# Attention scores and values as 64-row products on each half of TensorE's rows

## The chip, the cores and the metric

The kernel runs on one core of a Trainium2 chip. The time is the device time of one execution in microseconds (us), 590.46 us as the median of three runs before the change. The profile is of one further execution, taken by the hardware profiler. Its engines are called PE (TensorE's matmuls), PEld (TensorE's weight loads, which overlap matmuls), DVE (VectorE), ACT (ScalarE), POOL (GpSimd) and SP (SyncE, which here issues DMAs).

## The reference, cut to what matters

Attention with keys and values averaged over 8 neighbouring positions is followed by a mixture of 8 experts, of which each token takes one. The second part isn't touched.

```python
B, H, S, D = (8, 8, 576, 64); Sp = 72
k_p = k.reshape(B, H, Sp, 8, D).mean(axis=3)
v_p = v.reshape(B, H, Sp, 8, D).mean(axis=3)
scores = q @ k_p.T / sqrt(D)                 # 576 x 72 for each of 64 heads
attn = softmax(scores)
x = (attn @ v_p)  ->  (B * S, H * D) = (4608, 512)
e = argmax(x @ w_gate + modality_bias[modality_id])
out = softmax value of e  *  relu(x @ w1[e]) @ w2[e]
```

All of it is in float32. A matmul of float32 operands that is not a transpose shows in the trace as two records of weight load and matmul; a transpose shows as one of each.

## The kernel before, in words

The first 172 us are the attention, the rest is the experts, which begin as the last attention steps end. Attention handles 36 tiles of 128 tokens. Two tiles make a step (`steps`, 16 of them); besides, there are four mixed steps of one tile, which holds the last 64 tokens of one batch and the last 64 of the next. Each step does its eight heads in two parts `w` of four heads.

For a step and a part, `q_pe` transposes q. It takes two tokens' 64 dimensions at once, so that in `qt` rows 0 to 63 hold one token's dimensions and rows 64 to 127 the other's: `qt` has two 128-token tiles stacked on the 128 rows that the matmul sums over. The keys `kt` are therefore kept twice, once with zeros in rows 64 to 127 and once with zeros in rows 0 to 63 (`kt[:, 0]` and `kt[:, 1]`, 576 columns each). `s_pe` (L586 to L604) multiplies, for each of four heads, `qt` (128 rows, 128 columns as weights) with both copies side by side: 128 rows, 2 x 72 = 144 columns. Half of the operand is zeros.

`s_dve` takes row maxima and subtracts them, `s_act` takes the exponentials and sorts them: per tile and pair of heads 128 of the 144 columns go to one 128-column block of `pe` (main), the other 16 to a tail. `t_pe` and `t_act` transpose the four blocks of a tile to `pt`, `t4_pe` and `t4_act` transpose the tails of the step and copy rows 0 to 63 to `pt4z[0]` and rows 64 to 127 to `pt4z[1]`; the other rows of these stay zero.

`a_pe` (L653 to L671) multiplies per pair of heads a block of `pt` with `vw`, whose columns are 2 x 73: for each head of the pair 64 value columns, 8 columns of the router's product and one column of ones, with zeros in the rows of the other head (`m_a` and `m_b` are the masks; row 72 is where the second head begins). Two products of `pt4z` with `v4` add the tails. That is 4 + 2 products of 128 rows and 146 columns for a tile. In mixed steps each product is done twice, for 64 tokens each, on one half of TensorE's columns.

`load_v`, `pool_v` and `v_operand` bring the values into this layout; `v_gate` makes the router's columns (L459, and L460 for the tails, which has 64 rows).

Nothing reorders the work: each engine does its instructions in the order in which the program's loop over steps (L980 to L1062) writes them. In that order the products stand between transposes: `t_pe`, `s_pe` of the second part, `t4_pe`, `a_pe`, `q_pe`, `s_pe` of the next step's first part. SP issues all loads in the order of a table, in one queue, and waits there for the tile that a load overwrites to be free.

## Time and profile before

| what | us |
|---|---|
| median of 3 runs (lowest, highest) | 590.46 (590.09, 590.72) |
| the profiled execution | 590.98 |
| its span, first to last instruction | 589.3 |
| PE, PEld busy | 570.9, 499.6 |
| DVE, ACT, POOL busy | 372.7, 273.8, 187.2 |

The span is 1.7 us shorter than the execution's time. The granted TensorE clock is 0.998 over the span. Matmuls overlap: one of 144 columns is shown with 289 ns though the next starts 0.12 us later, so a PE that reads as busy can still have lost time between two products. Rows of groups give busy time in us, the mean duration of one in ns, and the engine's idle time before them. `128*128 128x144` means weights on 128 rows and 128 columns, and a moving operand of 128 rows and 144 columns; `64*128` are weights on 64 rows.

### The profile page before, as it was taken

How to read it: one execution, taken by the hardware profiler on the slowest of the kernel's cores; microseconds unless marked ns; L12 is line 12 of the kernel's file. 1: busy time of each engine (PE TensorE's matmuls, PEld its weight loads, DVE VectorE, ACT ScalarE, POOL GpSimd, SP SyncE). 2: the span in 40 equal slices, each digit the busy share in tenths (PEclk: the TensorE clock that was granted, in tenths of full speed). 3: DMA queues.
4: the chain of work that ended last, by engine and by line, in shares of the span. 5: the costliest groups of instructions: out<-in, count | busy, mean ns of one | idle time of the engine just before them, and what ended most of it. 6: DMA issues, size and time to landing. Idle time of an engine off the chain costs nothing.

```text
span 589.3 us, 12333 instructions
## 1 busy us (share of the span) xinstructions
PE 570.9 (97%) x3539; PEld 499.6 (85%) x3539; DVE 372.7 (63%) x945; ACT 273.8 (46%) x652; POOL 187.2 (32%) x290
## 2 busy tenths in 40 slices
PE   6999999999999999999999999999999999999995
PEld 5789789988898888888888888888888888888894
DVE  5877898788966766557455446855455487555311
ACT  2767677788552333333333336633333474334210
POOL 7679967765000323112112102112102113212101
PEclk9999999999999999999999999999999999999999
DMA  8999979995311744232232277242234843241101
GB/s 257 306 323 282 360 219 309 304 313 171 103 54 39 263 169 121 79 125 91 82 118 95 86 230 241 91 125 91 87 111 137 255 158 105 91 146 54 38 3 55
DMA packets 83426, 92.60 MB, mean 157 GB/s; under 512 B 17871, under 2 KB 58319, under 8 KB 83344
## 3 DMA queue, kind: packets, MB, share of 16 engines
q1 hardware_dynamic: 77424, 72.24, 39.2%
q0 software_dynamic: 5920, 19.44, 9.9%
q8 instruction: 30, 0.49, 0.4%
q14 instruction: 52, 0.43, 0.2%
HBM read 123.06 MB, written 27.58 MB: 256 GB/s over the span
## 4 chain that ended last, share of the span: by engine, by line
PE 82%; DVE 7%; DMA 5%; ACT 2%; issue 1%; SPq 1%; POOLq 0%; POOL 0%; DVEq 0%; ACTq 0%
PE op L1345 33%; PE hp L209 20%; PE hp L214 10%; PE av L667 4%; PE hp L183 3%; PE sc L603 3%; DMA q<-in_q_dram 3%; PE av L671 2%; DMA v<-in_v_dram 2%; PE pp L632 2%; PE pq L578 2%; PE ph L183 1%; DVE mx L610 1%; DVE hl L141 1%; DMA out_dram<-obw,slw 1%
## 5 line engine op out<-in xcount | busy, mean ns | idle before, releaser
L209 PE MATMUL hp<-xhl,hl 128*128 128x512 f32 x512 | 126.6, 390 | 0.0
L1321 POOL DMA_INDIRECT out_dram<-ob,sidx x34 | 36.8, 1083 | 263.6 <-DVE ob L1315 191.2
L209 PEld LDWEIGHTS hp<-xhl,hl 128*128 128x128 f32 x512 | 96.1, 188 | 19.9
L217 ACT COPY ht<-hp 128x256 f32<-128x256 f32 x128 | 47.3, 373 | 138.7 <-PE hp L214 112.3
L218 DVE TENSOR_TENSOR ht<-ht,hp 128x256 f32<-128x256 f32 x128 | 52.8, 420 | 92.5 <-ACT ht L217 89.4
L1345 PE MATMUL op<-hl,hx 128*128 128x512 f32 x429 | 104.8, 392 | 0.0
L1345 PEld LDWEIGHTS op<-hl,hx 128*128 128x128 f32 x429 | 78.5, 189 | 14.6
L1345 PE MATMUL op<-hl,hh 128*128 128x512 f32 x256 | 79.8, 393 | 0.0
L214 PEld LDWEIGHTS hp<-xhl,hl 128*128 128x128 f32 x512 | 69.8, 191 | 4.9
L214 PE MATMUL hp<-xhl,hl 128*128 128x256 f32 x512 | 71.5, 283 | 0.0
L1345 PEld LDWEIGHTS op<-hl,hh 128*128 128x128 f32 x256 | 46.0, 189 | 7.8
L667 PE MATMUL av<-vw,pt 128*128 128x146 f32 (+1 forms) x320 | 49.2, 293 | 1.4 <-DVE xb L700 1.3
L1345 PE MATMUL op<-hl,hlo 128*128 128x512 f32 x128 | 49.9, 390 | 0.0
L144 POOL DMA_INDIRECT xg<-xs,gidx x36 | 38.6, 1073 | 29.0 <-DMA raw<-in_moe_w_dram 13.8
L667 PEld LDWEIGHTS av<-vw,pt 128*128 128x128 f32 (+1 forms) x320 | 39.6, 180 | 3.4 <-DVE xb L700 1.0
L223 DVE SCALAR_TENSOR_TENSOR hx<-ht,hx 128x256 fp32r<-128x256 f32 x64 | 27.2, 427 | 18.8 <-DVEq L1350 15.7
L223 DVE SCALAR_TENSOR_TENSOR hlo<-ht,hh 128x256 fp32r<-128x256 f32 x64 | 27.1, 425 | 18.5 <-DVEq L1350 15.3
L603 PE MATMUL sc<-kt,qt 128*128 128x144 f32 x256 | 37.4, 289 | 0.6 <-DVE rs L798 0.3
L603 PEld LDWEIGHTS sc<-kt,qt 128*128 128x128 f32 x256 | 33.2, 190 | 1.6 <-DVE rs L798 0.5
L610 DVE TENSOR_REDUCE mx<-sc 128x8 f32<-128x576 f32 (+1 forms) x40 | 27.7, 692 | 7.5 <-PE sc L603 6.9
L671 PE MATMUL av<-vw,pt 128*128 128x146 f32 (+1 forms) x160 | 30.0, 290 | 0.0
L221 ACT ACTIVATE hx<-ht 128x256 fp32r<-128x256 f32 x64 | 26.2, 419 | 7.4 <-DVE ht L218 5.7
(279 smaller groups left out, 907.7 us busy)
## 6 DMA issues: line engine op xcount, KB each, us to landing
raw<-in_moe_w_dram SPq DMA_DIRECT2D x288, 256.0 KB
xs<-xb SPq DMA_DIRECT2D x16, 528.0 KB
scr<-xg SPq DMA_DIRECT2D x29, 256.0 KB
k<-in_k_dram SPq DMA_DIRECT2D x7, 1024.0 KB
v<-in_v_dram SPq DMA_DIRECT2D x7, 1024.0 KB
q<-in_q_dram SPq DMA_DIRECT2D x7, 1024.0 KB
y<-scr SPq DMA_DIRECT2D x108, 64.0 KB
v<-in_v_dram SPq DMA_DIRECT2D x16, 128.0 KB
```

The costliest lines, as they stand in the source:

```text
L144: nc.gpsimd.indirect_dma_start(out=x, out_offset=None, in_=xs[0:rows, :], in_offset=IndirectOffsetOnAxis(idx[:, col:col + 1].bitcast(U32), 0),
L209: nc.tensor.matmul(hp[g % 2], hl[g][:, 0, d * P:(d + 1) * P], ab[:, d, :, 0:SLOT], start=(d == 0), stop=False)
L214: nc.tensor.matmul(hp[g % 2][:, 0:SLOT], hl[g][:, 1, d * P:(d + 1) * P], ab[:, d, 0, 0:SLOT], start=False, stop=(d == ND - 1))
L217: nc.scalar.copy(hts[g % 2], hp[g % 2][:, SLOT:2 * SLOT])
L218: nc.vector.tensor_add(hts[g % 2], hts[g % 2], hp[g % 2][:, 0:SLOT])
L223: nc.vector.scalar_tensor_tensor(hlo, hts[g % 2], 0.0, hh.bitcast(F32), op0=ALU.max, op1=ALU.subtract)
L603: nc.tensor.matmul(dst, qt[:, i, :], kt[b % NB][:, :, h * SPL:(h + 1) * SPL], start=True, stop=True)
L610: nc.vector.reduce_max(mx, scv, axis=AX.X)
L667: nc.tensor.matmul(av[hs, u, 2 * VC * gg:2 * VC * (gg + 1)], pt[:, c, hs], vw[y][:, c].rearrange("p a x -> p (a x)"), start=(gg == 0), sto ...
L671: nc.tensor.matmul(dst4[hs], pt4[:, hs], v4[y][:, 2 * u:2 * u + 2, :], start=False, stop=True)
L1321: nc.gpsimd.indirect_dma_start(out=out[:, :], out_offset=IndirectOffsetOnAxis(idx.bitcast(U32), 0), in_=ob, in_offset=None, bounds_check=N ...
L1345: nc.tensor.matmul(ot, l[:, ts_], hl[f][:, w, D:2 * D], start=(f == 0 and n == 0), stop=(f == NF - 1 and n == 2))
```

## The change

`kt` and `vw` lose their zero halves. `kt` holds the same keys in rows 0 to 63 and in rows 64 to 127. `s_pe` makes two products where there was one: rows 0 to 63 of `qt` with rows 0 to 63 of `kt`, and rows 64 to 127 with rows 64 to 127, of 72 columns each, into different banks of PSUM (index `a`). For the values a pair is now head `c` and head `4 + c`: the first 64 of a head's 72 pooled positions lie on one half of the rows, and the last 8 in the tail. `a_pe` makes 8 products of 64 rows and 73 columns, and for the tails two of 64 rows and 4 x 73 = 292 columns. In mixed steps products have 64 rows and 64 weight columns, so that four of them cover the array. The two halves stand next to each other in the program.

With that, loads of `v` are cut in two (64 rows each) and those of the tails in four; `v_operand` has one copy instead of two scaled ones; the transposed tails are written with a mask (`m_z`) to both `pt4z` in full height; memsets of `kt` and `pt4z` go away.

PE around `s_pe` of a step's second part (one step of two tiles; `pp` are transposes of the exponentials, `sc` the scores and, at L644 or L645, the transposed tails, `pv` transposes of pooled values, `av` the values' products), before:

```order
L632 MATMUL pp_771<-ident,pe_676 128x128 x4
L603 MATMUL sc_1_781<-kt_133,qt_1_709 128x2x72 x4
L644 MATMUL sc_0_729<-ident,pe_676 128x128
L443 MATMUL pv_792<-ident,vp_658 128x128 x2
L444 MATMUL pv_792<-ident,vp_2_659 64x128
L667 MATMUL av_800<-vw_137,pt_776 128x146 x2
L671 MATMUL av_800<-vw_139,pt_0_134 128x2x73
L667 MATMUL av_800<-vw_137,pt_776 128x146 x2
L671 MATMUL av_800<-vw_139,pt_0_134 128x2x73
```

and of the change:

```order
L634 MATMUL pp_844<-ident,pe_730 128x128 x4
L602 MATMUL sc_1_854<-kt_137,qt_1_775 128x72 x8
L645 MATMUL sc_0_795<-ident,pe_730 128x128
L443 MATMUL pv_868<-ident,vp_712 128x128 x2
L444 MATMUL pv_868<-ident,vp_2_713 64x128
L668 MATMUL av_876<-vw_141,pt_849 128x73 x8
L673 MATMUL av_876<-vw_143,pt_0_138 128x292 x2
```

The order of the groups is the same. Four products of scores became eight, six of values became ten, and the transposes of 128 rows before, between and behind them stayed where they were.

ACT at the same place (`pt_0` and `pt_1` are the two `pt4z`), before:

```order
L651 COPY pt_0_134<-sc_0_729 64x128
L651 COPY pt_1_135<-sc_0_729 64x128
L436 ACTIVATE vw_136<-vp_658,m_a 128x4x64
L437 ACTIVATE vw_136<-vp_658,m_b 128x4x64
L447 COPY vt_796<-pv_792 128x256
```

and of the change:

```order
L652 ACTIVATE pt_0_138<-sc_0_795,m_z_144 128x128
L652 ACTIVATE pt_1_139<-sc_0_795,m_z_145 128x128
L437 COPY vw_140<-vp_712 128x4x64
L447 COPY vt_872<-pv_868 128x256
```

Two copies of 64 rows became scaled ones of 128 rows, and two scaled copies became one plain one.

The diff, cut to its core:

```diff
--- before.py
+++ after.py
@@ -265,17 +265,20 @@
-        def load_v(b, pairs=slice(0, NPAIR)):
+        def load_v(b, pairs=slice(0, 4)):
             if b not in vraw:
                 vraw[b] = big.tile([P, NPAIR, POOL * HD], F32, tag=f"s{V_SLOT[b % 3]}", name=f"v_{b}")
-            src = rows_of(v, b).rearrange("(c r) x -> r c x", r=2 * SPL)[0:P]
-            nc.sync.dma_start(vraw[b][:, pairs], src[:, pairs, :])
+            src = rows_of(v, b).rearrange("(h r) x -> r h x", r=SPL)[0:64]
+            for a in range(2):
+                nc.sync.dma_start(vraw[b][64 * a:64 * a + 64, pairs], src[:, 4 * a + pairs.start:4 * a + pairs.stop, :])
         def load_v4(b):
             t4 = ap.tile([P, POOL * HD], F32, tag="v4", bufs=2, name=f"v4_{b}")
-            src = rows_of(v, b).rearrange("(c r) x -> r c x", r=2 * SPL)[P:]
-            for z in range(2):
-                nc.sync.dma_start(t4[64 * z:64 * z + 64], src)
+            src = rows_of(v, b).rearrange("(h r) x -> r h x", r=SPL)[64:]
+            for a in range(2):
+                for z in range(2):
+                    r0 = 64 * a + 32 * z
+                    nc.sync.dma_start(t4[r0:r0 + 32], src[:, 4 * a:4 * a + 4, :])
             v4raw[b] = t4
         def load_q(b, parts=(0, 1)):
@@ -302,32 +305,30 @@
...
-        load_v(0, slice(2, NPAIR))
+        load_v(0, slice(2, 4))
...
-        kt = [ap.tile([P, 2, H * SPL], F32, name=f"kt{i}") for i in range(NB)]
+        kt = [ap.tile([P, H * SPL], F32, name=f"kt{i}") for i in range(NB)]
         pt4z = [ap.tile([P, P], F32, name=f"pt4_{z}") for z in range(2)]
-        vw = [ap.tile([P, NPAIR, 2, VC], F32, name=f"vw{i}") for i in range(NB)]
+        vw = [ap.tile([P, NPAIR, VC], F32, name=f"vw{i}") for i in range(NB)]
...
-        m_a = ap.tile([P, 1], F32, name="m_a")
-        m_b = ap.tile([P, 1], F32, name="m_b")
+        m_z = [ap.tile([P, 1], F32, name=f"m_z{z}") for z in range(2)]
...
-            nc.gpsimd.memset(pt4z[z][64 - 64 * z:128 - 64 * z], 0.0)
         for i in range(NB):
-            nc.gpsimd.memset(kt[i][0:64, 1, :], 0.0)
-            nc.gpsimd.memset(kt[i][64:128, 0, :], 0.0)
-            nc.gpsimd.tensor_copy(vw[i][:, :, 0, VC - 1], m_a.to_broadcast([P, NPAIR]))
-            nc.gpsimd.tensor_copy(vw[i][:, :, 1, VC - 1], m_b.to_broadcast([P, NPAIR]))
+            nc.gpsimd.memset(vw[i][:, :, VC - 1:VC], 1.0)
...
@@ -401,8 +402,8 @@
...
             x = slice(cs[0] * P, cs[0] * P + n)
-            nc.scalar.copy(dst[0:64, 0, x], pk[:, 0:n])
-            nc.scalar.copy(dst[64:128, 1, x], pk[:, 0:n])
+            nc.scalar.copy(dst[0:64, x], pk[:, 0:n])
+            nc.scalar.copy(dst[64:128, x], pk[:, 0:n])
         def pool_v(b):
             vp = ap.tile([P, NPAIR, HD], F32, tag="vp", bufs=2, name=f"vp_{b}")
@@ -433,8 +434,7 @@
         def v_operand(b):
...
             dw, d4 = vw[b % NB], v4[b % NB]
-            nc.scalar.activation(dw[:, :, 0, 0:HD], vp, AF.Copy, scale=m_a)
-            nc.scalar.activation(dw[:, :, 1, 0:HD], vp, AF.Copy, scale=m_b)
+            nc.scalar.copy(dw[:, :, 0:HD], vp)
...
@@ -457,10 +457,13 @@
...
-            nc.tensor.matmul(pg[:, 2, :], vt4, wg[0:64, 1::2, :], start=True, stop=True)
+            for a in range(2):
+                hs = slice(64 * a, 64 * a + 64)
+                nc.tensor.matmul(pg[hs, 2, :], vt4[:, hs], wg[0:64, 4 * a:4 * a + 4, :], start=True, stop=True)
             pgv = pg[:, 0:2, :].rearrange("p u (g a e) -> p (u g) a e", g=2, a=2)
-            nc.scalar.activation(dw[:, :, 0, HD:HD + E], pgv[:, :, 0, :], AF.Copy, scale=m_a)
-            nc.scalar.activation(dw[:, :, 1, HD:HD + E], pgv[:, :, 1, :], AF.Copy, scale=m_b)
+            for a in range(2):
+                hs = slice(64 * a, 64 * a + 64)
+                nc.scalar.copy(dw[hs, :, HD:HD + E], pgv[hs, :, a, :])
...
@@ -589,18 +592,15 @@
...
             if jj is None:
-                for u in range(2):
-                    c = 2 * w + u
-                    for z in range(2):
-                        hs = slice(64 * z, 64 * z + 64)
-                        src = kt[(b - 1 + z) % NB].rearrange("p a (h s) -> p (a h) s", s=SPL)[:, 2 * c:2 * c + H + 2:H + 1, :]
-                        nc.tensor.matmul(sc[hs, u, 0:2 * SPL].rearrange("p (a s) -> p a s", a=2), qt[:, u, hs], src,
-                                         start=True, stop=True)
+                tiles = [(u, slice(64 * z, 64 * z + 64), (b - 1 + z) % NB, 4 * w + 2 * u, 1) for u in range(2) for z in range(2)]
             else:
-                for i in range(4):
-                    dst = sc[:, i // 2, 0:4 * SPL].rearrange("p (t x) -> p t x", t=2)[:, :, (i % 2) * SPL:(i % 2 + 1) * SPL]
-                    h = 4 * w + i
-                    nc.tensor.matmul(dst, qt[:, i, :], kt[b % NB][:, :, h * SPL:(h + 1) * SPL], start=True, stop=True)
+                tiles = [(i, slice(0, P), b % NB, 4 * w + i, 0) for i in range(4)]
+            for i, hs, y, h, step in tiles:
+                for a in range(2):
+                    rows = slice(64 * a, 64 * a + 64)
+                    x = (h + step * a) * SPL
+                    nc.tensor.matmul(sc[hs, a, i * SPL:(i + 1) * SPL], qt[rows, i, hs], kt[y][rows, x:x + SPL],
+                                     start=True, stop=True)
             scs[n, w] = spare[w] = sc
         def s_dve(n, w):
@@ -619,11 +619,13 @@
...
             pe, sb = pes[n], scs.pop((n, w))
-            sv = sb[:, :, 0:2 * nt * SPL].rearrange("p u (t x) -> p u t x", t=nt)
-            main = pe[:, 0:2 * NPAIR * P].rearrange("p (t x) -> p t x", t=2)[:, 0:nt, 2 * w * P:2 * (w + 1) * P]
-            tail = pe[:, 2 * NPAIR * P:].rearrange("p (t s c) -> p t c s", t=2, c=NPAIR)[:, 0:nt, 2 * w:2 * w + 2, :]
-            nc.scalar.activation(main.rearrange("p t (u x) -> p u t x", u=2), sv[:, :, :, 0:P], AF.Exp, scale=escale)
-            nc.scalar.activation(tail.rearrange("p t u x -> p u t x"), sv[:, :, :, P:2 * SPL], AF.Exp, scale=escale)
+            main = pe[:, 0:2 * NPAIR * P].rearrange("p (t c a x) -> p t c a x", t=2, c=NPAIR, a=2)[:, :, :, w]
+            tail = pe[:, 2 * NPAIR * P:].rearrange("p (a t s c) -> p a t c s", a=2, t=2, c=NPAIR)[:, w]
+            if nt == 1:
+                main, tail = (x[:, 0].rearrange("p (c u) s -> p u c s", u=2) for x in (main, tail))
+            sv = sb[:, :, 0:2 * nt * SPL].rearrange("p u (c s) -> p u c s", s=SPL)
+            nc.scalar.activation(main, sv[:, :, :, 0:64], AF.Exp, scale=escale)
+            nc.scalar.activation(tail, sv[:, :, :, 64:SPL], AF.Exp, scale=escale)
         def t_pe(t):
             n, z = tile_step[t]
@@ -639,16 +641,15 @@
         def t4_pe(n):
-            m = 64 * len(steps[n][2])
-            dst = spare[0][0:m, 0, 4 * SPL:4 * SPL + P]
-            nc.tensor.transpose(dst, pes[n][:, 2 * NPAIR * P:2 * NPAIR * P + m], ident)
+            dst = spare[0][:, 0, 4 * SPL:4 * SPL + P]
+            nc.tensor.transpose(dst, pes[n][:, 2 * NPAIR * P:2 * NPAIR * P + P], ident)
             pt4s[n] = dst
         def t4_act(n):
             dst = pt4s[n]
             for z in range(len(steps[n][2])):
-                nc.scalar.copy(pt4z[z][64 * z:64 * z + 64], dst[64 * z:64 * z + 64])
+                nc.scalar.activation(pt4z[z], dst, AF.Copy, scale=m_z[z])
         def a_pe(t):
             n, z = tile_step[t]
@@ -660,15 +661,17 @@
...
                 halves = [(slice(64 * y, 64 * y + 64), (b - 1 + y) % NB) for y in range(2)]
-            for u in range(2):
-                for gg in range(2):
-                    c = 2 * u + gg
-                    for hs, y in halves:
-                        nc.tensor.matmul(av[hs, u, 2 * VC * gg:2 * VC * (gg + 1)], pt[:, c, hs],
-                                         vw[y][:, c].rearrange("p a x -> p (a x)"), start=(gg == 0), stop=False)
-                dst4 = av[:, u, 0:4 * VC].rearrange("p (g x) -> p g x", g=2)[:, :, VC:2 * VC]
+            for a in range(2 * NPAIR):
+                c, a = a // 2, a % 2
+                rows = slice(64 * a, 64 * a + 64)
                 for hs, y in halves:
-                    nc.tensor.matmul(dst4[hs], pt4[:, hs], v4[y][:, 2 * u:2 * u + 2, :], start=False, stop=True)
+                    nc.tensor.matmul(av[hs, a, VC * c:VC * (c + 1)], pt[rows, c, hs], vw[y][rows, c, :],
+                                     start=(c == 0), stop=False)
+            for a in range(2):
+                rows = slice(64 * a, 64 * a + 64)
+                for hs, y in halves:
+                    nc.tensor.matmul(av[hs, a, 0:4 * VC], pt4[rows, hs], v4[y][rows].rearrange("p c x -> p (c x)"),
+                                     start=False, stop=True)
         def x_dve(t):
             n, z = tile_step[t]
```

More of the change, by code (lines that the diff above doesn't have):

```diff
@@ L304 @@
         load_q(0, (1,))
-        load_v(0, slice(2, NPAIR))
+        load_v(0, slice(2, 4))
         NB = 2
-        kt = [ap.tile([P, 2, H * SPL], F32, name=f"kt{i}") for i in range(NB)]
+        kt = [ap.tile([P, H * SPL], F32, name=f"kt{i}") for i in range(NB)]
         pt4z = [ap.tile([P, P], F32, name=f"pt4_{z}") for z in range(2)]
-        vw = [ap.tile([P, NPAIR, 2, VC], F32, name=f"vw{i}") for i in range(NB)]
+        vw = [ap.tile([P, NPAIR, VC], F32, name=f"vw{i}") for i in range(NB)]
         v4 = [ap.tile([P, NPAIR, VC], F32, name=f"vw4{i}") for i in range(NB)]
-        m_a = ap.tile([P, 1], F32, name="m_a")
-        m_b = ap.tile([P, 1], F32, name="m_b")
+        m_z = [ap.tile([P, 1], F32, name=f"m_z{z}") for z in range(2)]
         m_4 = ap.tile([P, NPAIR], F32, name="m_4")
-        nc.vector.tensor_single_scalar(m_a, iota_p, float(SPL), op=ALU.is_lt)
-        nc.vector.tensor_single_scalar(m_b, iota_p, float(SPL), op=ALU.is_ge)
-        nc.scalar.activation(m_4[:, 0:1], m_a, AF.Exp)
+        nc.vector.tensor_single_scalar(m_4[:, 0:1], iota_p, float(SPL), op=ALU.is_lt)
+        nc.scalar.activation(m_z[0], m_4[:, 0:1], AF.Exp)
+        m_j = ap.tile([P, 1], I32, name="m_j")
+        nc.gpsimd.iota(m_j, pattern=[[0, 1]], base=0, channel_multiplier=1)
+        nc.vector.tensor_single_scalar(m_j, m_j, 32, op=ALU.bitwise_and)
+        for z in range(2):
+            nc.vector.tensor_single_scalar(m_z[z], m_j, 32.0 * z, op=ALU.is_equal)
         m_i = ap.tile([P, NPAIR], I32, name="m_i")
@@ L343, in gate_operand @@
             for g in range(2):
-                nc.gpsimd.tensor_copy(wgb[64 * g:64 * g + 64, :, g, :],
-                                      wg[64 * g:64 * g + 64].rearrange("p (u g a) e -> p u g (a e)", u=2, g=2)[:, :, g, :])
+                nc.gpsimd.tensor_copy(wgb[64 * g:64 * g + 64, :, g, :].rearrange("p u (a e) -> p u a e", a=2),
+                                      wg[64 * g:64 * g + 64].rearrange("p (a u g) e -> p u g a e", a=2, u=2)[:, :, g])
         kps, vps, vts = {}, {}, {}
```

1 line of the change is left out of this document (removed).

## The prediction

> **What bounds the kernel now.** I read the page first, then the busy times of the attention stage, then the chain of waits in it, and last the timeline of PE around the two kinds of products.
>
> ```profile
> span 589.3 us, 12333 instructions
> PE 570.9 (97%) x3539; PEld 499.6 (85%) x3539; DVE 372.7 (63%) x945; ACT 273.8 (46%) x652; POOL 187.2 (32%) x290
> ```
>
> ```profile
> 15.00:165.00 150.00, 143.34 (x1222) 130.78 (x1221) 126.69 (x350) 107.98 (x291) 96.91 (x161) 1.00 0.85 265
> ```
>
> ```profile
> by line: PE av L667 13.8%; PE sc L603 10.7%; DMA q<-in_q_dram 10.1%; PE av L671 6.5%; DMA v<-in_v_dram 5.8%; PE pq L578 5.6%; PE pp L632 5.5%; DVE mx L610 4.2%; DVE hl L141 3.8%; DVE sb L613 3.5%; issue 3.1%; DVE xb L700 3.0%; PE ph L183 2.
> ```
>
> The first row gives the busy times of PE, PEld, DVE, ACT and POOL from 15 to 165 us, then the clock (1.00), the DMA engines' share (0.85) and GB/s. The second is the chain of waits from 15 to 172 us by line. PE is busy 143 of 150 us, DVE 127: PE bounds the stage, with DVE close behind. Scores and values (L603, L667, L671) are 31% of the chain. Of 157 us that is about 49.
>
> ```profile
> ACT pt L637 <- PE pp L632: 13.1, 10, 1.6
> DVE r L690 <- PE av L671: 11.4, 20, 1.3
> ...
> PE av L667 <- DVE xb L700: 1.3, 2, 0.7
> ```
>
> These waits (total us, times, longest) up to 200 us say the same: DVE and ACT wait for PE far more than PE waits for them.
>
> **The change part by part: what one product costs.** A product of 128 rows and 144 columns is two records, and all of them come in blocks:
>
> ```profile
> 72.83 1.15 PE L603 MATMUL sc<-kt,qt 128*128 128x144 f32 x8
> 73.82 0.60 PE L578 MATMUL pq<-ident,q 128*128 128x128 f32 x4
> 74.25 0.67 PE L667 MATMUL av<-vw,pt 128*128 128x146 f32 x4
> ...
> 75.75 0.60 PE L632 MATMUL pp<-ident,pe 128*128 128x128 f32 x4
> ```
>
> Eight records of scores take 73.82 - 72.83 = 0.99 us, 0.123 each; a tile's twelve of values 75.75 - 74.25 = 1.50, 0.125 each. No time is lost where they meet the transposes. Whether such a record costs its moving columns or its weight load, the mixed steps and the gate product tell:
>
> ```profile
> 102.66 0.44 PE L578 MATMUL pq<-ident,qm 128*128 128x128 f32 x2
> 103.03 0.71 PE L597 MATMUL sc<-kt,qt 128*64 128x144 f32 x8
> 103.67 0.65 PE L578 MATMUL pq<-ident,q 128*128 128x128 f32 x4
> 104.16 0.53 PE L459 MATMUL sc<-wgb,vt 128*128 128x32 f32 x4
> 104.62 0.41 PE L460 MATMUL sc<-wg,vt 64*128 64x32 f32 x2
> 104.96 0.77 PE L667 MATMUL av<-vw,pt 128*128 128x146 f32 x4
> ...
> 105.81 0.66 PE L667 MATMUL av<-vw,pt 128*128 128x146 f32 x4
> ...
> 106.56 0.60 PE L632 MATMUL pp<-ident,pe 128*128 128x128 f32 x4
> ```
>
> ```profile
> 103.03 0.44 PEld L597 LDWEIGHTS sc<-kt,qt 128*64 128x64 f32 x8 [0.17 <-issue]
> 103.67 0.42 PEld L578 LDWEIGHTS pq<-ident,q 128*128 128x128 f32 x4 [0.20 <-issue]
> 104.06 0.53 PEld L459 LDWEIGHTS sc<-wgb,vt 128*128 128x128 f32 x4
> 104.62 0.29 PEld L460 LDWEIGHTS sc<-wg,vt 64*128 64x128 f32 x2
> ```
>
> ```profile
> L603 PEld LDWEIGHTS sc<-kt,qt 128*128 128x128 f32 x256 | 33.2, 190 | 1.6 <-DVE rs L798 0.5 <-ACT qt L584 0.4 <-issue 0.4
> ...
> L597 PEld LDWEIGHTS sc<-kt,qt 128*64 128x64 f32 x64 | 3.7, 136 | 1.7 <-ACT vg L467 0.7 <-issue 0.7 <-DVE sb L613 0.2
> ...
> L459 PEld LDWEIGHTS sc<-wgb,vt 128*128 128x128 f32 x28 | 3.7, 192 | 0.0
> ...
> L460 PEld LDWEIGHTS sc<-wg,vt 64*128 64x128 f32 x14 | 2.1, 185 | 0.3
> ```
>
> First, halves of columns run at once: eight records of L597 with 144 columns take 0.64 us (103.03 to 103.67), where one after another they would take 0.99. Second, weight loads have a pace of their own. L459 moves only 32 columns, and its loads start (0.53 - 0.19) / 3 = 0.113 us apart; those of L460, with 64 rows, 0.29 - 0.185 = 0.105 apart. So a load of 128 columns takes about 0.11 us whether 128 or 64 rows are filled, and one of 64 columns 0.190 - 0.136 = 0.054 us less. Third, going to another tile shape and back costs time. In the rows of PEld no load is issued for 0.17 us ahead of L597 and 0.20 behind it, with no semaphore named.
>
> The **round trip** in two ways. L578 before L597 begins its second transpose at 102.66 + 0.44 - 0.28 = 102.82, and transposes follow each other at (0.60 - 0.28) / 3 = 0.11; the one after L597 runs 0.05 us late (0.65 for four instead of 0.60). From 102.93 to 103.72 are 0.79 us for four pairs of records at 0.123, so 0.30 are lost. For L460: L459's last begins at 104.16 + 0.53 - 0.28 = 104.41, the next could have begun at 104.52, and L667 begins effectively at 104.96 + (0.77 - 0.66) = 105.07; less two loads at 0.11, 0.33 are lost. With weights of 128 columns the first load, which nothing covers, is 0.054 longer than in L597: I take 0.30 + 0.05 = 0.35 us.
>
> **The sum.** The trace shows no two halves of rows in use at once. The nearest row is L597, two halves of columns at once, so I take them to run at once, bounded by the load at 0.11 us for a pair, since 72 columns move in half of 0.123, 0.06 us.
>
> - Scores of a full step: 8 pairs, of which the first load is in the round trip: 7 x 0.11 + 0.06 + 0.35 = 1.18 us instead of 0.99, +0.19. There are 32 such blocks (256 records of L603, 8 each).
> - Values of a full tile: 8 x 0.11, then the tails, 292 columns in two pairs of 2 x 0.125 us, as long as before, then 0.35: 1.73 us instead of 1.50, +0.23. 32 tiles.
> - Together 32 x 0.42 = 13.4 us. Seven of the value blocks follow L460 and three of the score blocks follow a transpose of 64 rows, so that their way in was paid before: 10 x 0.17 off, 11.7.
> - Mixed steps paid the round trip already. Four products cover the array, at 0.06 us for four: scores 4 x 0.06 instead of 4 x 0.123, -0.24 in each of 8 blocks; values 8 x 0.06 + 2 x 0.25 instead of 12 x 0.123, -0.50 in each of 4. That is -1.9 - 2.0 = -3.9.
>
> PE gets 7.8 us more work. Of the 79 us of full blocks (32 x 0.99 + 32 x 1.50), 49 lie on the chain, 62%; where the chain runs over DVE or the loads of q, the extra is covered by what PE waits there. 0.62 x 7.8 = +4.8 us.
>
> The Trainium skill states the concurrency itself (TensorE: Matmul & The Clock Gate, Part 3): products in different row groups run at once, at the duration of one plus some 4 ns for each further one. By that a pair would cost 0.114, not 0.11, and the sum would be 32 x 0.06 = 1.9 us of PE work higher; no run here shows it yet.
>
> The bounds of a block: with a round trip of 0.30 and loads at 0.105, +0.11 and +0.14, PE 32 x 0.25 - 1.5 - 3.9 = +2.6 us; with a round trip of 0.42 and pairs no faster than a record is today, 0.123, +0.35 and +0.40, PE 24 - 2.1 - 3.9 = +18 us.
>
> **ACT** gets less to do.
>
> ```profile
> L651 ACT COPY pt<-sc 64x128 f32<-64x128 f32 x36 | 9.5, 264 | 0.4
> ...
> L436 ACT ACTIVATE vw<-vp,m_a 128x256 f32<-128x256 f32 x8 | 4.1, 511 | 0.3
> L437 ACT ACTIVATE vw<-vp,m_b 128x256 f32<-128x256 f32 x8 | 4.0, 498 | 0.0
> ...
> L447 ACT COPY vt<-pv 128x256 f32<-128x256 f32 x8 | 3.0, 369 | 0.3 <-PE pv L444 0.2
> ...
> L463 ACT ACTIVATE vw<-sc,m_b 128x32 f32<-128x32 f32 x7 | 2.0, 285 | 0.0
> L467 ACT COPY vg<-sc 128x32 f32<-128x32 f32 x7 | 1.3, 186 | 0.0
> ```
>
> A scale costs about 0.1 us (L463 against L467, 285 and 186 ns), so the 36 copies of tails get +0.1 each, +3.6. Each of 8 batches saves 0.511 + 0.498 - 0.369 = 0.64 in `v_operand` and 0.2 in `v_gate`: -6.7. ACT has 42 us to spare of 150, so I count 0; were all of it on the path, it would be between +3.6 and -6.7. POOL loses six memsets ahead of a wait for v: 0. DVE keeps its shapes: 0.
>
> **SP** issues more loads, and the first ones count:
>
> ```profile
> 3.85 1.23 SPq L278 DMA_DIRECT2D v<-in_v_dram  x2
> 5.13 0.59 SPq L272 DMA_DIRECT2D v<-in_v_dram  x1
> ...
> 6.27 0.51 SPq L272 DMA_DIRECT2D v<-in_v_dram  x1
> ```
>
> ```profile
> 6.27 9.14 DMA v<-in_v_dram
> ```
>
> Two more for the tails, one more for each part of v, at some 0.5 us: the last is issued 2 us later. Queued behind it in SP are the gate's weights and the next keys. The chain shows 9.14 us from that issue to its landing, most of it spent behind the same bytes as before. I take 0; were the issue the limit, +2 us.
>
> All terms: 4.8 us onto the profiled execution's 590.98 us (span 589.3) are 595.8; the median of the runs is 0.5 lower, so 595.3. I say **595 us**.
>
> **Rivals.**
>
> *The two halves of rows load one after another.* Then every record costs a load. Scores 15 x 0.11 + 0.06 + 0.35 = 2.06, +1.07; values 16 x 0.11 + 0.50 + 0.35 = 2.61, +1.11: 32 x 2.18 - 1.7 = +68 us of PE work, more than any cover, about 650 us after what waits give back. For it: the rows show only one half of the rows in use. Against: L597's two halves load at once.
>
> *Faster: half the rows load in half the time.* A pair would be bounded by its 72 columns, 0.06 us. Scores 7 x 0.06 + 0.06 + 0.30 = 0.78, -0.21; values 8 x 0.06 + 0.50 + 0.30 = 1.28, -0.22: -13.8 - 1.5 - 3.9 = -19 us of PE. With DVE at 127 of 150 us only a third to 0.62 of it would come out: -6 to -12, so 582. It decides below a pair time of about 0.09 us. For it: 31% of the chain are these lines. Against: L460's loads at 0.105 us. The Trainium skill promises up to twice the speed where the contraction is 64 rows or fewer (TensorEngine Tiling (Array Packing), Theoretical Speedup), which would be this rival's result; L460's loads speak against that.
>
> *All of it is hidden.* PE's extra goes into its waits for DVE, ACT and q, and the time stays at 590 to 591.5. For it: DVE at 127 of 150 and loads at 0.85 of the DMA engines' time. Against: the waits quoted above.
>
> **How the numbers follow.** Forecast 0.66, with its own range from 592 (the cheap bound, 0.4 of it coming out) to 604 (the dear bound, 0.75 of it); loads one after another 0.11; faster 0.09; hidden 0.14. A range of 588 to 604 holds the forecast's share of 0.65 and the hidden one's 0.14, and a little of the faster one; 650 us is left out. A measurement of this kernel tells 0.2%, 1.2 us, from no change: faster 0.11 (0.09 and an edge of the hidden case), same 0.14, slower 0.75.
>
> **What would show it.** Right: score blocks of 16 records between 1.1 and 1.3 us, their loads in pairs that start together and 0.11 us apart; PEld idle for 0.17 us or more on both sides without a semaphore; mixed blocks shorter. PE's attention ends 4 to 8 us later, the experts' stage keeps its length. Loads of the two halves that never start together would mean the first rival; pairs at 0.06 us the second; DVE or q waits that shrink by as much as PE gains, the third. I would be wrong if the stage ends earlier, or if what is lost stands in ACT or in the loads of v.

## The result and the profile after

The changed kernel takes 623.9 us as the median of six runs, 5.4% longer than before: a ratio of 1.0539 with a 95% interval from 1.0521 to 1.0557. I had forecast 595 us and a range up to 604. One plain word on the profile: it was taken of an execution of 637.04 us (span 635.2), longer than the undisturbed ones at 621 to 624, so its lengths are read against other stretches of itself, and sizes are taken from the timed runs.

The loss arises in the attention. The last product of values, in the timeline of PE, before and then after (start, duration, engine, line):

```profile
179.19 0.41 PE L671 MATMUL av<-vw,pt 128*128 128x146 f32 x2
```

```profile
225.07 0.71 PE L673 MATMUL av<-vw,pt 64*128 64x292 f32 x4
```

It ends at 179.60 before and at 225.78 after, 46.2 us later; the two profiled executions differ by 637.04 - 590.98 = 46.1. The experts' stage keeps its length.

From the page of after, the span, the busy times, the granted clock of PE in 40 slices (9 is 90% or more) and the queue of SP's loads:

```profile
span 635.2 us, 13683 instructions
...
PE 600.8 (95%) x4195; PEld 504.0 (79%) x4195; DVE 370.4 (58%) x947; ACT 272.5 (43%) x644; POOL 183.7 (29%) x283
...
PEclk9588699798896999999999999999999999999999
...
q1 hardware_dynamic: 77568, 72.24, 40.9%
```

The same two rows of before:

```profile
PEclk9999999999999999999999999999999999999999
...
q1 hardware_dynamic: 77424, 72.24, 39.2%
```

The queue moves the same 72.24 MB, but its packets hold the DMA engines longer: 40.9% of 635.2 us is 259.8, 39.2% of 589.3 is 231.0, 12% more time for the same bytes. And PE, at full clock throughout before, has slices at 0.5 to 0.9 of it in the first third of the span. The stretches of the attention, after (busy times of PE, PEld, DVE, ACT and POOL, then clock, DMA share, GB/s):

```profile
15.00:60.00 45.00, 35.37 (x343) 27.93 (x343) 24.84 (x51) 19.81 (x54) 22.55 (x40) 0.75 1.03 208
60.00:105.00 45.00, 38.46 (x408) 30.75 (x409) 24.58 (x70) 21.82 (x61) 32.06 (x53) 0.83 0.93 249
105.00:150.00 45.00, 42.61 (x534) 33.55 (x532) 32.02 (x101) 28.35 (x78) 27.78 (x46) 0.92 0.85 233
150.00:180.00 30.00, 28.37 (x285) 22.36 (x281) 19.84 (x62) 21.76 (x56) 12.60 (x22) 0.83 0.74 242
```

and before:

```profile
15.00:60.00 45.00, 42.53 (x349) 38.85 (x348) 35.46 (x78) 31.32 (x87) 35.16 (x62) 1.00 1.03 306
60.00:105.00 45.00, 43.09 (x367) 39.28 (x365) 39.40 (x117) 30.80 (x85) 35.66 (x60) 1.00 0.93 299
105.00:150.00 45.00, 44.25 (x387) 40.51 (x387) 37.52 (x116) 38.20 (x102) 26.09 (x40) 1.00 0.79 258
150.00:180.00 30.00, 28.46 (x249) 27.14 (x248) 22.97 (x70) 14.76 (x37) 0.00 (x0) 1.00 0.16 51
```

From 15 to 60 us the DMA engines are as full as they were (1.03), but move 208 GB/s instead of 306. PE, PEld, DVE, ACT and POOL are all less busy there. From 150 to 180 us, where loading was nearly over before (51 GB/s), it still runs at 242. The longest waits for loads up to 215 us (total, times, longest), after:

```profile
PE pq L581 <- DMA q<-in_q_dram: 18.2, 3, 9.9
...
POOL v L352 <- DMA v<-in_v_dram: 16.1, 5, 7.9
...
POOL k L352 <- DMA k<-in_k_dram: 15.6, 4, 8.4
...
DVE vp L357 <- DMA v<-in_v_dram: 7.4, 1, 7.4
```

and before:

```profile
POOL k L351 <- DMA k<-in_k_dram: 5.0, 2, 3.0
...
POOL v L351 <- DMA v<-in_v_dram: 4.1, 3, 2.3
...
PE pq L578 <- DMA q<-in_q_dram: 1.7, 2, 1.1
```

The chain of waits of after over the first 60 us is for the most part loads of v, one behind the other (start, us):

```profile
11.28 10.57 DMA v<-in_v_dram
21.88 12.92 DMA v<-in_v_dram
35.50 17.89 DMA v<-in_v_dram
```

Meanwhile the products did what I had said. Where the clock is full, PE and then PEld of after read:

```profile
125.35 1.12 PE L668 MATMUL av<-vw,pt 64*128 64x73 f32 x16
126.30 0.71 PE L673 MATMUL av<-vw,pt 64*128 64x292 f32 x4
126.94 0.66 PE L634 MATMUL pp<-ident,pe 128*128 128x128 f32 x4
127.43 0.60 PE L581 MATMUL pq<-ident,q 128*128 128x128 f32 x4
127.96 1.11 PE L602 MATMUL sc<-kt,qt 64*128 64x72 f32 x16
129.01 0.44 PE L581 MATMUL pq<-ident,qm 128*128 128x128 f32 x2
```

```profile
126.94 0.42 PEld L634 LDWEIGHTS pp<-ident,pe 128*128 128x128 f32 x4 [0.39 <-issue]
...
127.96 0.97 PEld L602 LDWEIGHTS sc<-kt,qt 64*128 64x128 f32 x16 [0.17 <-issue]
```

Sixteen loads in 0.97 us are eight pairs (0.97 - 0.19) / 7 = 0.111 us apart, and in the trace's records the two of a pair start 0.007 us after each other: two halves of rows load together, at the pace of one. PEld issues nothing for 0.17 us ahead of the block, without a semaphore. From its start to the next product the scores block takes 1.05 us (0.99 before). Before it, the four transposes of q need 127.96 - 127.43 = 0.53 instead of the 0.43 of before; so the block costs 1.15, where I had 1.18. The values take 126.94 - 125.35 = 1.59 instead of 1.50, with a way in and out on top; I had 1.73 with both.

### The profile page after: what moved, and what is told of

It reads as the page before. It is cut to its first block, busy times and chain, and to the rows that moved or that the text cites. A ratio compares the mean times of both kernels' runs of the same rounds, so it can differ in the third digit from the quotient of the medians.

```text
span 635.2 us, 13683 instructions
## 1 busy us (share of the span) xinstructions
PE 600.8 (95%) x4195; PEld 504.0 (79%) x4195; DVE 370.4 (58%) x947; ACT 272.5 (43%) x644; POOL 183.7 (29%) x283
## 3 DMA queue, kind: packets, MB, share of 16 engines
q1 hardware_dynamic: 77568, 72.24, 40.9%
## 4 chain that ended last, share of the span: by engine, by line
PE 78%; DMA 17%; issue 2%; SPq 1%; POOL 1%; ACT 1%; DVE 0%; POOLq 0%; ACTq 0%; DVEq 0%
PE op L1348 31%; PE hp L209 18%; PE hp L214 10%; DMA v<-in_v_dram 8%; DMA q<-in_q_dram 4%; PE av L668 4%; DMA k<-in_k_dram 3%; PE sc L602 3%; PE hp L183 3%; PE av L673 2%; PE pp L634 2%; PE ph L183 2%; PE pq L581 1%; DMA out_dram<-obw,slw 1%; PE xt L173 1%
## 5 line engine op out<-in xcount | busy, mean ns | idle before, releaser
L602 PE MATMUL sc<-kt,qt 64*128 64x72 f32 (+1 forms) x640 | 46.2, 296 | 0.6 <-issue 0.4
L602 PEld LDWEIGHTS sc<-kt,qt 64*128 64x128 f32 (+1 forms) x640 | 39.8, 200 | 8.7 <-issue 6.6
L668 PE MATMUL av<-vw,pt 64*128 64x73 f32 (+1 forms) x640 | 43.9, 291 | 2.4 <-DVE xb L703 1.4
L668 PEld LDWEIGHTS av<-vw,pt 64*128 64x128 f32 (+1 forms) x640 | 38.4, 197 | 8.7 <-ACT pt L652 3.0
L581 PE MATMUL pq<-ident,q 128*128 128x128 f32 x128 | 25.3, 330 | 20.4 <-DMA q<-in_q_dram 18.2
L581 PEld LDWEIGHTS pq<-ident,q 128*128 128x128 f32 x128 | 17.2, 167 | 26.2 <-issue 15.7
```

The source lines that it names most:

```text
L581: nc.tensor.transpose(pq[:, c, :], src, ident)
L602: nc.tensor.matmul(sc[hs, a, i * SPL:(i + 1) * SPL], qt[rows, i, hs], kt[y][rows, x:x + SPL], start=True, stop=True)
L668: nc.tensor.matmul(av[hs, a, VC * c:VC * (c + 1)], pt[rows, c, hs], vw[y][rows, c, :], start=(c == 0), stop=False)
```

## The experiments

Theory at the start: the loads of v and of its tails cost the time, since they go to fewer rows at once, and PE's slow clock follows its waits for them. Rivals: the products of 64 rows themselves, with a clock that they pull down; the number of loads that SP issues; the time that one queue needs. The microseconds behind a ratio are that ratio less one, of 590.5 us.

**The loads of v alone, halved.**

```diff
-            nc.sync.dma_start(vraw[b][:, pairs], src[:, pairs, :])
+            for a in range(2):
+                nc.sync.dma_start(vraw[b][64 * a:64 * a + 64, pairs], src[64 * a:64 * a + 64, pairs, :])
```

> The kernel before, with nothing changed but that each load of v for 128 rows is issued as two loads of 64 rows. No product is changed. Theory L (loads): the changed kernel lost its time because a load into 64 rows moves its bytes at about half the pace, and the stage is bound by loads. Packets of 2 KB took 84 to 105 ns there before and about 160 after; v is 8 MB, and at the 310 GB/s of the stage before that is some 27 us, so twice that price is at most +27 us, and what prefetch hides comes off: 605 to 618 us, with waits for v, k and q on POOL, DVE and PE, and a granted clock under 0.99. Theory P (products): the round trips between tile shapes and the lowered clock come from the 64-row products: 590 to 592 us here, clock 0.998.

Measured: 1.0324 [1.0279, 1.0369], +19 us, without any product changed. Two stretches of this run, 4 us each, columns as above:

```profile
44.00:48.00 4.00, 0.22 (x2) 0.01 (x1) 2.45 (x3) 1.06 (x3) 3.69 (x7) 0.94 1.09 243
48.00:52.00 4.00, 3.09 (x14) 3.12 (x15) 0.00 (x0) 1.70 (x4) 3.61 (x8) 0.50 1.00 185
```

PE does nothing for nearly 4 us while the DMA engines are full, and in the next 4 us its clock is 0.50. So the slow clock can come with late loads alone, without any product of 64 rows. The Trainium skill (TensorE: Matmul & The Clock Gate, Part 1) states a half clock after some 3.4 us of idling; this trace agrees.

**The tails alone, in four loads of 32 rows** (each from 8 source rows of the four pairs of heads).

```diff
-                nc.sync.dma_start(t4[64 * z:64 * z + 64], src)
+                for y in range(2):
+                    r0 = 64 * z + 32 * y
+                    nc.sync.dma_start(t4[r0:r0 + 32], src[8 * y:8 * y + 8])
```

> The kernel before, with nothing changed but that the tails of v come in four loads of 32 rows, the source walked as 8 rows of 4 heads, instead of two of 64 rows from 16 rows of 4 pairs. Theory T (tails): loads with 8 as their slowest size use half of the 16 DMA engines, which then carry 2 MB more of the stage's 34 MB than their share, so every later load lands late: 594 to 600 us. Theory L in its narrow form (only the 64-row loads of 512 KB matter) and theory P: 590 to 592 us.

Measured: 1.0067 [1.0045, 1.0089], +4 us, though the tails are a quarter of the bytes of the main loads (2 x 128 KB for a batch against 1 MB).

```profile
15.00:60.00 45.00, 41.66 (x316) 38.14 (x317) 32.37 (x69) 29.50 (x81) 31.90 (x55) 0.92 0.96 283
```

This loss looks different from that of the halves. Less is moved (283 GB/s instead of 306), but the DMA engines are also less busy (0.96 instead of 1.03). A load leaves marks in the trace as its parts land: one of 128 rows or of 64 leaves sixteen, each of these leaves eight when it lands and one early. That fits the theory of the tails, by which such a load is carried by half of the DMA engines. The height is not the reason: 32 neighbouring rows cost what 64 do (below).

**All loads of the change, no product of it**: the two edits above together.

> The kernel before, with all the loads of the changed kernel: v in two 64-row loads, its tails in four of 32 rows. No product is changed. If the loads are nearly all of the loss: 591.3 + 19 + 4.5 = 615 us or some more, since both slow the same engines, up to 621; the granted clock falls as in the changed kernel, though no product has 64 rows. If the products and the loads make each other worse: not above 612 us.

Measured: 1.0437 [1.0407, 1.0467], +26 us of the +32. From 15 to 60 us the pace is nearly that of after (217 GB/s, there 208), but the clock is 0.91, there 0.75:

```profile
15.00:60.00 45.00, 30.93 (x227) 26.96 (x227) 24.94 (x51) 20.52 (x56) 25.28 (x44) 0.91 1.04 217
```

The difference is how long a slow stretch lasts. This run, first, is back at full clock within some 4 us; after, in the next two rows, stays near 0.50 for 21 us, and for 7 us with PE busy throughout and hardly a load under way:

```profile
48.00:52.00 4.00, 3.78 (x29) 3.35 (x29) 1.98 (x6) 0.00 (x0) 3.42 (x6) 0.57 1.07 351
52.00:56.00 4.00, 1.55 (x11) 1.14 (x9) 3.08 (x6) 1.94 (x5) 2.29 (x6) 1.00 1.08 161
```

```profile
17.00:38.00 21.00, 18.80 (x117) 15.13 (x117) 9.59 (x17) 6.96 (x19) 10.36 (x19) 0.51 1.07 225
113.00:120.00 7.00, 7.00 (x48) 5.38 (x48) 3.65 (x15) 3.08 (x10) 0.68 (x2) 0.53 0.27 65
```

By the clock's records in the traces, after is at 0.50 in five stretches of 6.8 to 20.5 us, 68 us together; this run in five of 3.4 to 6.8 us, 24 us together. It is not only this one profile: the mean clock of the executions of after at 621 to 624 us is 0.951 to 0.964, that of this run's four is 0.971 to 0.985. So the late loads start a slow stretch, and with the products of 64 rows it lasts longer. Why is not shown.

**The reverse: all products of the change, with the loads of before.** The values then stand at other positions, so the routing of tokens and with it the experts' stage differ; only the attention can be compared.

```diff
-            src = rows_of(v, b).rearrange("(h r) x -> r h x", r=SPL)[0:64]
-            for a in range(2):
-                nc.sync.dma_start(vraw[b][64 * a:64 * a + 64, pairs], src[:, 4 * a + pairs.start:4 * a + pairs.stop, :])
+            src = rows_of(v, b).rearrange("(c r) x -> r c x", r=2 * SPL)[0:P]
+            nc.sync.dma_start(vraw[b][:, pairs], src[:, pairs, :])
...
```

> The changed kernel, with the loads of v and of its tails as they were before. The rows of v then stand where the changed products do not expect them, so the values are those of other positions; the amount of work and its order are those of the changed kernel. Theory L or T: the time falls back to what the products alone cost, which my sum had as +2 to +8 us: 592 to 599 us, clock above 0.99. Theory P: it stays above 612 us with a clock near 0.96.

```profile
15.00:60.00 45.00, 42.84 (x524) 33.82 (x522) 34.87 (x74) 29.90 (x82) 35.07 (x63) 1.00 1.03 311
```

The last product of values, in the timeline:

```profile
181.65 0.71 PE L670 MATMUL av<-vw,pt 64*128 64x292 f32 x4
```

The pace (311 GB/s) and the clock (1.00) are back, and the attention ends at 182.36, 2.8 us later than before. That is one execution of each: the profiles of four kernels below that lose nothing (mixed scores, pairs, even rows, every fourth row) end their attention between 178.8 and 181.5, so the products alone cost some 1 to 4 us of it. The whole execution took 1.0394 [1.0344, 1.0444], outside both of the expected ranges: what follows the attention takes 429 us instead of 410, with the tokens routed otherwise.

**Only the scores of full steps as products of 64 rows**, and **only those of mixed steps**, on the kernel before. The core of the first, and of the second:

```diff
-                    nc.tensor.matmul(dst, qt[:, i, :], kt[b % NB][:, :, h * SPL:(h + 1) * SPL], start=True, stop=True)
+                    for a in range(2):
+                        rows = slice(64 * a, 64 * a + 64)
+                        nc.tensor.matmul(sc[:, a, i * SPL:(i + 1) * SPL], qt[rows, i, :],
+                                         kt[b % NB][rows, a, h * SPL:(h + 1) * SPL], start=True, stop=True)
```

```diff
-                        nc.tensor.matmul(sc[hs, u, 0:2 * SPL].rearrange("p (a s) -> p a s", a=2), qt[:, u, hs], src,
-                                         start=True, stop=True)
+                        for a in range(2):
+                            rows = slice(64 * a, 64 * a + 64)
+                            x = (2 * c + a) * SPL
+                            nc.tensor.matmul(sc[hs, a, u * SPL:(u + 1) * SPL], qt[rows, u, hs],
+                                             kt[(b - 1 + z) % NB][rows, a, x:x + SPL], start=True, stop=True)
```

> The kernel before, with only the scores of full steps as 64-row products (kt keeps its two copies, the halves of the rows write two banks, the order of columns in the exponentials is kept by a view). Loads and values as before. My sum: 32 blocks at +0.19 us, three of which had paid their way in, +5.6 us of PE work, 0.62 of it coming out: +3.5, 594 us. Theory P with the clock: a block of 64-row products lowers the granted clock, and the time is over 600 us. If PE's waits cover it all: 590 to 591.5 us.

> The kernel before, with only the scores of the four mixed steps as products of 64 rows and 64 columns, four of them over the array. Loads, values and the other scores as before. These blocks pay their way in and out already, and my sum had -0.24 us for each of 8: -1.9 us of PE work, 0.62 of it coming out: -1.2, 589.5 to 590.5 us against 591.3. If PE's waits decide: no change, within 0.2%.

Measured: 1.0034 [1.0008, 1.0059], +2.0 us where my sum gave +3.5; and 1.0004 [0.9988, 1.0021], nothing where it gave -1.2. In the run with all products and whole loads a mixed block reads:

```profile
104.40 0.48 PE L599 MATMUL sc<-kt,qt 64*64 64x72 f32 x16
104.98 0.66 PE L578 MATMUL pq<-ident,q 128*128 128x128 f32 x4
```

Its row of PEld:

```profile
104.40 0.33 PEld L599 LDWEIGHTS sc<-kt,qt 64*64 64x64 f32 x16 [0.17 <-issue]
```

It takes 0.58 us instead of the 0.64 of before (103.03 to 103.67): a gain of 0.06, not 0.24. The loads themselves need 0.33.

**Is it the number of loads?** Two loads of 128 rows, half of the pairs each:

```diff
-            nc.sync.dma_start(vraw[b][:, pairs], src[:, pairs, :])
+            m = (pairs.start + pairs.stop) // 2 if pairs.start else pairs.stop // 2
+            for part in (slice(pairs.start or 0, m), slice(m, pairs.stop)):
+                nc.sync.dma_start(vraw[b][:, part], src[:, part, :])
```

> The kernel before, with each load of v issued as two again, but each of 128 rows and half the heads. It has as many loads of v, of the same bytes, as the run with 64-row halves. If it is the height of the load that costs (64 rows reach only some of the ways into the memory): 590 to 592 us. If it is the number of loads, or what SP pays to issue them: 605 to 613 us, as with the halves.

Measured: 0.9989 [0.9970, 1.0009]. It is not.

**Is it the one queue?** Rows 0 to 63 from SP, rows 64 to 127 from ACT:

```diff
-            nc.sync.dma_start(vraw[b][:, pairs], src[:, pairs, :])
+            for a, queue in enumerate((nc.sync, nc.scalar)):
+                queue.dma_start(vraw[b][64 * a:64 * a + 64, pairs], src[64 * a:64 * a + 64, pairs, :])
```

> The kernel before, with v in two 64-row halves, rows 0 to 63 issued by SP and rows 64 to 127 by ACT, so that the two halves can be under way side by side. If one half alone is slow because it reaches half of the ways into the memory, both together reach all: most of the 19 us comes back, 592 to 600 us, the rest being what ACT pays to issue. If a 64-row load is slow in itself: 605 to 613 us or more.

Measured: 1.0276 [1.0234, 1.0319]. Two halves side by side do not recover the pace. The Trainium skill advises against splitting a load by halves of rows over two queues, since both use the same engines (DMA: Bandwidth & Descriptors, Rules for kernel authors); this run agrees.

**Which rows, or how many?** From here every kernel is the one before with each load of v cut in another way. Even and odd rows:

```diff
+            for a in range(2):
+                nc.sync.dma_start(vraw[b][a::2, pairs], src[a::2, pairs, :])
```

> The kernel before, with each load of v in two of 64 rows again, but the even rows in one and the odd rows in the other. Packets (2 KB), their number, the number of loads and the rows of each are those of the run with rows 0 to 63 and 64 to 127 (ratio 1.0324). Theory 'which rows': a load is slow because its rows lie in one half of SBUF, and even rows reach all of it: ratio 0.998 to 1.004, 590 to 593 us, about 300 GB/s from 15 to 60 us. Rival 'how many rows': any load of 64 rows is slow: ratio 1.025 to 1.035, 606 to 612 us, about 260 GB/s.

Measured: 0.9998 [0.9978, 1.0018]. Loads of 64 rows with the same packets cost nothing if their rows spread over all 128. The stretch of the halves, and then of this run:

```profile
15.00:60.00 45.00, 38.09 (x295) 34.63 (x293) 29.63 (x61) 27.41 (x74) 28.37 (x51) 0.92 1.07 260
15.00:60.00 45.00, 43.21 (x355) 39.50 (x354) 36.06 (x80) 31.76 (x89) 35.86 (x64) 1.00 1.04 320
```

Every fourth row, four loads of 32 rows (`a::4`), against four of 32 neighbours (`32 * a:32 * a + 32`):

> The kernel before, with each load of v in four of 32 rows, each with every fourth row. The run with even and odd rows lost nothing (0.9998); the one with rows 0 to 31, 32 to 95 and 96 to 127 lost 3.0% where half of 3.2% was forecast. Theory 'which rows' alone: 32 rows that are spread over all of SBUF cost nothing, ratio 0.998 to 1.004, 590 to 593 us. Rival: loads of 32 rows are slow in themselves, which would account for the 3.0%: ratio 1.01 or more, 597 us or more.

> The kernel before, with each load of v in four of 32 neighbouring rows. If in the run with rows 0 to 31, 32 to 95 and 96 to 127 the middle load went at full pace and the outer two, 32 rows each, lost 3.0% between them, four such loads lose twice that: ratio 1.05 to 1.065, 620 to 629 us. If 32 neighbouring rows cost what 64 do, and the middle load was as slow as the rest: ratio 1.028 to 1.038, 607 to 614 us.

Measured: 1.0013 [0.9992, 1.0035], and 1.0307 [1.025, 1.0364]. Which rows decides, and 32 neighbours cost what 64 do.

The marks of landing say the same of single loads. The middle of a load's marks, less that of the load ahead of it in the full queue, is about the time that it took. On the mean, 512 KB took 1.52 us as half of the pairs in 128 rows, 1.46 as even or odd rows, and 2.53 as 64 neighbouring rows; a whole load of 1 MB before took 2.99. Two halves are thus 2.1 us slower than one whole load; over eight batches that is an estimated 17 us, near the 19 measured.

**Reading or writing?** Source rows 0 to 63 and 64 to 127, written to the even and the odd rows; and the reverse:

```diff
+                nc.sync.dma_start(vraw[b][a::2, pairs], src[64 * a:64 * a + 64, pairs, :])
```

```diff
+                nc.sync.dma_start(vraw[b][64 * a:64 * a + 64, pairs], src[a::2, pairs, :])
```

> The kernel before, with each load of v in two of 64 rows: the source rows are neighbours (0 to 63 and 64 to 127 of the 128), the rows written in SBUF are the even ones and the odd ones. The values stand at other positions, so the routing of the tokens and the experts' stage differ; what is compared is the attention stage alone. Theory 'rows of SBUF': the rows written decide, so nothing is lost: 295 to 325 GB/s from 15 to 60 us, last product of values at 178 to 182 us. Rival 'rows of DRAM': about 260 GB/s, last product at 190 to 196 us.

> The reverse: source rows even and odd, rows written in SBUF 0 to 63 and 64 to 127, again with values at other positions and the attention stage alone to be compared. Theory 'rows of SBUF': as slow as neighbours on both sides, about 260 GB/s from 15 to 60 us, last product of values at 190 to 196 us. Rival 'rows of DRAM': 295 to 325 GB/s, last product at 178 to 182 us.

The first, from 15 to 60 us:

```profile
15.00:60.00 45.00, 43.28 (x346) 39.61 (x344) 34.96 (x76) 31.61 (x86) 34.49 (x61) 0.96 1.04 307
```

and the second:

```profile
15.00:60.00 45.00, 33.58 (x243) 30.00 (x244) 24.94 (x51) 22.37 (x60) 27.25 (x48) 0.86 1.02 223
```

307 against 223 GB/s: the rows that are written in SBUF decide. The last product of values begins at 180.79 us in the first and at 197.82 in the second (179.19 before, 194.12 with halves on both sides). The whole executions, 1.0398 and 1.074, cannot be compared, as the tokens are routed otherwise. Whether reading from afar adds to the loss (223 GB/s where the halves gave 260) stays open: by the marks of landing 512 KB took 2.54 us, as in the halves.

**Neighbours, or one half of SBUF?** The even and the odd rows of each half, four loads:

```diff
+            for a in range(4):
+                rows = slice(64 * (a // 2) + a % 2, 64 * (a // 2) + 64, 2)
+                nc.sync.dma_start(vraw[b][rows, pairs], src[rows, pairs, :])
```

> The kernel before, with each load of v in four of 32 rows: the even and the odd rows of 0 to 63, the even and the odd rows of 64 to 127. The rows are no neighbours, but each load stays within one half of SBUF. Theory 'reach': a load is slow because its rows together reach only a part of SBUF's ports, and these rows lie in one half: ratio 1.025 to 1.037, 606 to 614 us. Rival 'neighbours': rows next to one another are slow to write, and stepping over every second one cures it: ratio 0.998 to 1.006, 590 to 595 us; the changed kernel could then be mended in the same way.

Measured: 1.0342 [1.0275, 1.041]. Stepping over rows within a half cures nothing, and the changed kernel, whose operands need a head's 64 rows side by side, can't be mended that way.

Rows 0 to 31, 32 to 95 and 96 to 127, three loads; and half of the pairs in halves, half in whole loads:

```diff
+            for r0, r1 in ((0, 32), (32, 96), (96, 128)):
+                nc.sync.dma_start(vraw[b][r0:r1, pairs], src[r0:r1, pairs, :])
```

```diff
+            mid = (pairs.start + pairs.stop + 1) // 2 if pairs.start else pairs.stop // 2
+            for r in (slice(0, 64), slice(64, P)):
+                nc.sync.dma_start(vraw[b][r, pairs.start or 0:mid], src[r, pairs.start or 0:mid, :])
+            nc.sync.dma_start(vraw[b][:, mid:pairs.stop], src[:, mid:pairs.stop, :])
```

> The kernel before, with each load of v in three: rows 0 to 31, 32 to 95, 96 to 127. Theory 'which rows': the middle load has 32 rows of either half of SBUF and goes at the full pace, the outer two are as slow as loads within one half; half of the bytes are slow, so about half of the loss of the two halves, ratio 1.010 to 1.020, 597 to 602 us. Rival 'how many rows': none has 128 rows, all are slow: ratio 1.03 or more, 609 us or more.

> The kernel before, with half of the pairs of each v loaded in two of 64 rows (0 to 63, 64 to 127) and the other half in one of 128 rows: half of the bytes go in loads that lie in one half of SBUF, as in the run with rows 0 to 31, 32 to 95 and 96 to 127, if its middle load was fast. If the loss goes with the bytes: ratio 1.012 to 1.020, 598 to 603 us, and then rows 32 to 95 were as slow as the rest. If half of the bytes already cost what all of them do, since loads behind them wait as long: ratio 1.026 to 1.034, 606 to 611 us, and the run with three loads fits the theory of reach.

Measured: 1.0298 [1.0271, 1.0324], and 1.0131 [1.0087, 1.0174]. By these ratios alone the three loads lose nearly all of 3.2%, the half of the bytes that is slow for certain less than half of it, and rows 32 to 95 would be as slow as the rest, though they lie in both halves. The traces say less. From 15 to 60 us, three loads and then half in halves:

```profile
15.00:60.00 45.00, 38.51 (x297) 35.04 (x296) 29.84 (x63) 27.37 (x74) 28.54 (x51) 0.92 1.05 259
15.00:60.00 45.00, 40.17 (x311) 36.68 (x310) 30.94 (x67) 28.29 (x76) 29.89 (x54) 0.93 1.04 265
```

The paces are alike, and in these two profiles the attention ends at 191.3 and 192.2 us. By the marks of landing, 512 KB in rows 32 to 95 took 2.07 us, between the 1.52 of full height and the 2.53 of a half. Part of that may come from the slow load just ahead: loads of full height right behind halves took 1.75. So the middle rows did not go at the full pace, and it is not shown that they are as slow as one half.

What the slow loads have in common is that their rows lie within 64 neighbouring ones; every load at full pace had rows from all of the 128.

The Trainium skill says that a load's pace goes by how many of 16 ports of SBUF its rows reach, that rows 0 to 63 reach eight, and that only one transfer that spans all rows reaches sixteen (SBUF — State Buffer, Door 1: The DMA port swizzle, and "Can I just issue two DMAs to hit both halves?"). The halves, the quarters and the spread rows agree with it. By the table of ports in the first of these sections rows 32 to 95 would reach all sixteen; 2.07 us where full height took 1.52 speaks against the full pace there, and why is open.

## Why the prediction was wrong

**The step that failed** is the one on SP. I wrote that the last load is issued 2 us later, that it waits "behind the same bytes as before", and "I take 0; were the issue the limit, +2 us". The bytes are the same and the issues cost nothing (0.9989 for two loads of whole height). But I priced a load by its bytes and its issue alone, and not by the rows that it writes nor by the way in which it is cut. Cut as the change cuts them, the loads cost 26 of the 32 us: 19 the halves of v alone, 4 the tails alone. Before already showed how little room there was: from 15 to 60 us its DMA engines were full, 1.03. I had quoted the mean of 0.85 from 15 to 165 us, which hides that in the first third of the attention the loads have nothing to spare. The trace of before has no load of v's main rows at half height that would have priced it, but it has a hint: its tails, 128 KB each in 64 rows, took 0.49 us by the marks of landing, where an eighth of a whole load's 2.99 is 0.37. The bound should have reached further than the issues. One of the prediction's own signs of being wrong, that what is lost stands in the loads of v, is what came.

**The clock**, too, was no term of my sum. PE waits for the late loads up to 9.9 us at a time, and comes back at half speed: over the 45 us from 15 to 60 the granted clock is 0.75, where it was 1.00. The loads start this: with whole loads and all new products the clock stays at 1.00 from 15 to 180 us. They do not account for all of it: with the new loads and the old products it is 0.91 from 15 to 60.

**The products** came as argued, and smaller. Halves of rows load at once, 0.111 us for a pair (0.11 forecast), with 0.17 us ahead of a block in which PEld issues nothing; a block of scores costs 1.15 (1.18). So the two rivals on that question, loads one after another (650 us) and pairs at half the time (582 us), fell. What comes out of it in the end was smaller: +4.8 us forecast, +2.8 measured in the attention of one execution with whole loads (1 to 4, as said); for the scores of full steps alone +2.0 [0.5, 3.5], with 3.5 in the sum. I had let 0.62 of PE's extra come out, the share of these blocks on the chain; it seems that more of it was covered, but the intervals reach up to the forecast. The mixed steps gain 0.06 us in a block of scores, not 0.24, and nothing that can be measured in the end: the sixteen loads need only 0.33 us, four at a time, but from their end to the next tile shape pass another 0.25, which I had counted as paid.

**What stays open** of the sum: 5.39% less 4.37% for the loads leaves 1.0%, 6 us (3 to 9 by the two intervals), for products that cost 2.8 us with whole loads. What they add on top of late loads was not separated; the longer stretches at half clock, 68 us instead of 24 in the two profiles, stand there and may be it.

**ACT, POOL, DVE** at 0 and the experts' stage at its old length were right: from 15 to 180 us DVE is busy for 101 us instead of 135, ACT 92 instead of 115, POOL 95 instead of 97, and none shows as a new limit; from the end of the attention to that of the span pass 409 us, as before (410). *All of it is hidden* was wrong for the reason above, though it held for the mixed steps. No version here beats the kernel before.

## What to carry to other kernels

A layout for TensorE's halves of rows is paid at the load: if the two halves hold things that are not evenly spaced in memory, each load writes 64 neighbouring rows, and 8 MB of v loaded so cost 3.2% here. Before cutting a load, look whether the stretch that it feeds has its DMA engines full (1.03 here), and cut it by columns or by every second row, which cost nothing here, not by height. Halving an operand that is half zeros gained nothing on PE here: a pair's weight load (0.11 us) bounded the product, and each block of another tile shape cost its way in and out.

## What the runs showed of the hardware that I had not expected

- Loads of v whose rows lie within 64 neighbouring rows of SBUF: 249 to 260 GB/s from 15 to 60 us instead of 302 to 320 for rows spread over all 128, at the same packets and full DMA engines; 32 rows cost what 64 do, and two queues recover little, if anything (2.8% lost instead of 3.2%). Rows 32 to 95 lie between: 2.07 us for 512 KB, where full height took 1.52 and a half 2.53.
- The pace depends on where rows are written, not where they are read (307 against 223 GB/s).
- Loads cut so that eight marks of landing come instead of sixteen lost 0.7% for a quarter of the bytes, with the DMA engines less busy (0.96 instead of 1.03).
- After PE was idle for nearly 4 us its granted clock was 0.50 in the next 4 us, so a late load costs more than its wait. With products of 128 rows the clock was back after 3.4 to 6.8 us; in the changed kernel it stayed at 0.50 for up to 20.5 us, at times with PE busy throughout.
